# One buffer class for outputs and relu results, one for inputs and inverse decays, three-chunk channel weights, and a new instruction order in a linear-attention plus mixer kernel

## The chip, the cores and the metric

The kernel runs on one core of one Trainium2 chip. The metric is the device time of one execution in microseconds (us), the median of several runs. The engines are named as in the profile: PE is TensorE, DVE is VectorE, ACT is ScalarE, POOL is GpSimd, SP is SyncE, which here only issues transfers. PEld is the weight load of TensorE.

## What is computed

A gated linear attention (a state that decays by `alpha` at each step) gives `x`; an MLP mixer, first over tokens and then over channels, follows. There are 4 batches, 8 heads of 48 and 768 time steps.

```python
for t in range(S):
    state = alpha[:, :, t, :, None] * state + np.einsum('bhd,bhe->bhde', k[:, :, t], v[:, :, t])
    y[:, :, t] = np.einsum('bhd,bhde->bhe', q[:, :, t], state)
...
h = np.maximum(xt @ w_tok1, 0.0) @ w_tok2          # 768 -> 256 -> 768 over tokens
u = x + h.transpose(0, 2, 1)
h2 = np.maximum(u @ w_ch1, 0.0) @ w_ch2            # 384 -> 1536 -> 384 over channels
return (u + h2).astype(np.float32)
```

## The kernel before

**Attention.** The 12 chunks of 256 time steps (3 to a batch, numbered 0 to 11, the last part of each step's name) are worked one after the other. A partition holds two successive steps. Of a chunk the four inputs `at` (alpha), `kt`, `qt` and `vt` are loaded by `ld_at`, `ld_kt`, `ld_qt`, `ld_vt`, 384 KB each. `ln` takes the logarithm, `cum` (in chunks 0 to 2 the wider `cumw`) sums it along the steps by matmul, `E` and `IE` are its exponential and the inverse of that, `kk` and `qq` scale the keys and queries by them, `trk`/`trq` transpose these on PE (chunks 0 to 5; later `dk`/`dq` do it by transfer) and `evk`/`evq` (`pq`) bring them to SBUF. `G` is the product of keys and queries for each half chunk (`G0_`, `G1_`), `mask` its causal mask on DVE, `K` the state's increment, made from the key copies `ka`, `kb`, `kc` and the value copies `vb`, `vs0_`, `vs1_`, `sa` and `sm` the new state, `ia`/`ib` the part of the output that comes from the state, `y` the rest, and `x` the copy of the result to SBUF.

**Mixer.** For each batch b, `t1_b_m_c` multiplies by `w_tok1`, `ht` is its relu, `t2_b_i` multiplies by `w_tok2`, `u_b_i` adds x, `up`/`ut` (batch 0) or the transfer `ux` (others) transposes u, `c1_b_mc_half` multiplies by `w_ch1` for one of 12 column chunks `mc` and one half of the time steps, `rt` is its relu, `c2_b_i_q` sums over `w_ch2` in four parts, `o_b_i` adds u, and `st_b_i` stores 128 steps. The weights come in as 16 loads `ldw` of 384 KB into the same buffers as the inputs, and a cast `cw` brings each to bf16: 2 of `wt1`, 2 of `wt2`, 6 of `wc1`, 6 of `wc2`.

**What sets the order.** `build` writes down every step with what it reads and writes. `ORDER` is a table of step names; the letter at a name's end is the engine (t PE, s ACT, v DVE, g POOL, y SP). Each engine runs its own steps strictly in the order in which they stand there. `BUFS` gives the number of the buffer for each value at its first use, within its class; `CLASSES` says how many each class has. A step waits by semaphores for what it reads and for the last user of a buffer that it overwrites. In `ORDER` a load stands shortly before its first reader, so it says nothing of when the load runs: SP runs through its loads, as far as buffers are free.

**Fillers.** Steps `fN_name` are matmuls on zeros with no use but to keep PE at work, worth N matmuls of 512 columns, put ahead of the step `name` in batch 0's stretch.

**A shared port.** Steps marked `port=True` (products on SBUF operands and casts) are chained over DVE and POOL: `shared` makes one of them on DVE wait for the last one before it on POOL in `ORDER`, and the other way round.

Lines that the profile names: L584 loads inputs, L600 to L607 the weights, L624 stores; L637/L631/L634 are the logarithms, L687/L679 `IE`, L683/L676 `E`; L700 `kk` and `qq`; L712 `trk`/`trq`; L643 is every other small matmul, fillers (`ps<-rt`) included; L746 and L745 copies and casts; L770 `mask`; L841 and L844 `sa` and `sm`; L878, L883, L902 and L907 are `t1`, `t2`, `c1` and `c2`; L875/L873 the relus; L887 `u`; L894 `up`; L911 `o`.

What a channel product waits for before is said by two lines: for chunks 0 to 5 three weight pieces, for chunks 6 to 11 the three others.

```python
reads=[ut], preds=(uts[0:2 + half] if b in UP else [uts[half]]) + [wl[("wc1", p)] for p in ((0, 1, 2) if mc < 6 else (3, 4, 5))],
```

Of the kernel before, what the change touches and what calls it, by code (L numbers as in the profile page):

```python
# [8 lines left out]
F32 = mybir.dt.float32  # L9
# [54 lines left out]
class Plan:  # L64
# [5 lines left out]
    def val(self, cls, name=""):  # L70
        return Val(cls, name)
# [30 lines left out]
UP = (0,)  # L102
# [5 lines left out]
    "in": 19,  # L108
    "la": 2, "lf": 2, "E": 3, "IE": 2, "pkq": 2, "pkk": 3, "vb": 3,
    "tpk": 4, "tpq": 2, "gtm": 2, "tmp": 2, "ss": 4, "kt": 1, "x": 9, "ht": 3, "u": 4, "ut": 2, "rt": 20, "o": 3,  # L110
}
WIDE = (0, 1, 2)
# [8 lines left out]
def build(g):  # L121
# [185 lines left out]
    wl = {}  # L307
# [8 lines left out]
    def mixer(b):  # L316
# [56 lines left out]
        for i in range(NS):  # L373
            hold = 4000.0 if (i >= NS - 3 and b < B - 1) else 0.0
            cuts = [(0, HD // 2), (HD // 2, HD)] if (b, i) == LAST else [(0, HD)]
            for ci, (ca, cz) in enumerate(cuts):
                nm = f"{b}_{i}" if len(cuts) == 1 else f"{b}_{i}h{ci}"
                bank, o_ = V("one"), V("o")
# [31 lines left out]
ld_at1y ld_at0y ln1s ln0s f8_cumw1t f1_cumw1t cumw1t IE1s cumw0t IE0s ld_vt0y E0s vb0g vs0_0g vs1_0v ld_kt0y kk0v  # L410
f8_trk0t f1_trk0t trk0t E1s ld_qt0y qq0v ka0s kb0s kc0v f1_trq0t trq0t ld_kt1y kk1v K0t evq0s s0_0v ld_vt1y vb1s
f1_trk1t trk1t ld_at2y evk0v ln2s f2_G0_0t G0_0t ld_qt1y ka1g sa1_0v f4_cumw2t cumw2t mask0_0v vs0_1s kb1g kc1g vs1_1s
K1t sm1_0g qq1v sa0_1v sm0_1v G1_0t ld_kt2y IE2s E2s trq1t evq1s ib0t mask1_0v f3_y1_0t y1_0t y0_0t evk1v G0_1t sa1_1v
ld_qt2y x1_0s mask0_1v G1_1t ld_vt2y x0_0s vb2s kk2g trk2t kc2s ldw_wt10y qq2g cw_wt10s f2_ia1t ia1t mask1_1v evk2s
trq2t ld_at3y vs1_2g ldw_wt11y evq2v ib1t y1_1t y0_1t vs0_2g ldw_wt21y sm1_1g P3g K2t sa0_2v sm0_2g x0_1s t1_0_0_0t
f1_G0_2t G0_2t ldw_wt20y G1_2t cw_wt20g t1_0_1_0t mask0_2v x1_1s t1_0_1_1t ld_at4y ld_kt3y t1_0_1_2t lnP3s cum3t
cw_wt11s IE3s ia2t y0_2t x0_2s t1_0_0_1t t1_0_0_2t E3s t1_0_0_3t mask1_2v t1_0_1_3t ib2t y1_2t ldw_wc14y t1_0_1_4t
x1_2s t1_0_0_4t f1_t1_0_1_5t t1_0_1_5t ht_0_1v P4g cw_wt21s t1_0_0_5t ht_0_0s f3_t2_0_0t t2_0_0t t2_0_1t u_0_0v ln13s
r13s ldw_wc13y t2_0_2t u_0_1v t2_0_3t u_0_2v t2_0_5t lnP4s t2_0_4t u_0_3v u_0_5v u_0_4v up_0_0t cw_wc14s cw_wc13s
# [74 lines left out]
class Emit:  # L494
# [76 lines left out]
    def t(self, v):  # L571
        return self.T[v.cls][v.buf]
# [393 lines left out]
```

## Time and profile before

| | us |
|---|---|
| median of 3 runs | 162.97 (162.54 to 163.51) |
| span of the profiled execution | 160.5 |
| PE busy in that span | 154.6 (96%) |
| DVE busy | 114.9 (72%) |
| ACT busy | 97.8 (61%) |
| POOL busy | 80.8 (50%) |
| c1, L902, 288 matmuls, busy | 50.3 |
| c2, L907, 300 matmuls, busy | 52.4 |
| fillers, L643 `ps<-rt`, 29 matmuls, busy | 12.1 |

The span goes from the first to the last instruction of the program in one profiled execution; the device time of a run also holds what lies around it. The ends of matmuls are modelled, so a small pause between two matmuls does not show as idle time; the difference of two starts does show it. HBM is read for 25.17 MB and written for 4.72 MB. Over the first 100 us the 16 transfer engines are busy nearly all the time, at some 320 GB/s.

### The profile page before, as it was taken

The page shows a single profiled execution, that of the slowest core. Times are in us where ns is not written, and L with a number is a line of the kernel's source. Part 1 is how long each engine was busy: PE and PEld are TensorE (multiplying, and loading weights), DVE is VectorE, ACT ScalarE, POOL GpSimd, SP SyncE. Part 2 cuts the span into 40 slices and gives each one's busy share as a digit, 9 for nine tenths or more (in the row PEclk, how much of TensorE's full clock was granted, in tenths as well). Part 3 has the DMA queues.
Part 4 walks back from the last instruction along what each step waited for, and adds up shares of the span by engine and source line. Part 5 has one row for each costly group of instructions (what it writes and reads, how often), then busy time and mean ns, then how long its engine had stood idle before and what let it go on. Part 6 is the DMA issues. An engine that isn't in the chain of part 4 may idle for free.

```text
span 160.5 us, 3971 instructions
## 1 busy us (share of the span) xinstructions
PE 154.6 (96%) x1563; PEld 97.1 (60%) x1563; DVE 114.9 (72%) x206; ACT 97.8 (61%) x179; POOL 80.8 (50%) x94
## 2 busy tenths in 40 slices
PE   7999989999999999999999999999999999999992
PEld 2545565766667676666667666566567665665661
DVE  6099994979889787989969758795886762464222
ACT  3789999998899955897563583269832203343000
POOL 5205897695973649389778852699523000000000
PEclk9999999999999999999999999999999999999999
DMA  4999999999999999999989999989701235111133
GB/s 122 320 324 317 317 374 311 339 333 306 316 347 324 275 278 272 210 228 319 241 202 298 239 315 204 217 196 134 196 21 62 87 79 169 49 49 53 49 129 116
DMA packets 76130, 35.05 MB, mean 218 GB/s; under 512 B 70352, under 2 KB 74320, under 8 KB 76112
## 3 DMA queue, kind: packets, MB, share of 16 engines
q1 hardware_dynamic: 73808, 31.76, 74.1%
q10 hardware_dynamic: 2304, 3.05, 5.3%
q8 instruction: 12, 0.20, 0.5%
q14 instruction: 6, 0.05, 0.1%
HBM read 25.17 MB, written 4.72 MB: 186 GB/s over the span
## 4 chain that ended last, share of the span: by engine, by line
PE 61%; DMA 12%; DVE 6%; ACT 6%; SPq 6%; POOL 4%; issue 3%; DVEq 0%; POOLq 0%
PE ps L907 22%; PE ps L902 21%; PE ps L643 11%; DMA in<-in_v_dram 6%; SPq L584 6%; DMA out_dram<-o 4%; PE ps L878 3%; PE ps L883 2%; DMA ut<-u 2%; DVE pkk L700 2%; DVE gtm L770 1%; PE ps L712 1%; DVE rt L875 1%; POOL vb L746 1%; POOL pkq L700 1%
## 5 line engine op out<-in xcount | busy, mean ns | idle before, releaser
L907 PE MATMUL ps<-wc,rt 128*128 128x384 bf16 (+1 forms) x300 | 52.4, 319 | 0.0
L902 PE MATMUL ps<-ut,wc 128*128 128x384 bf16 x288 | 50.3, 326 | 0.1
L902 PEld LDWEIGHTS <-wc 128*128 128x128 bf16 x288 | 27.1, 98 | 17.9 <-DMA ut<-u 0.6
L907 PEld LDWEIGHTS <-rt 128*128 128x128 bf16 x300 | 27.8, 98 | 16.0
L873 ACT ACTIVATE rt<-ps 128x384 bf16<-128x384 f32 x47 | 21.4, 492 | 23.6 <-PE ps L902 23.3
L875 DVE TENSOR_SCALAR rt<-ps 128x384 bf16<-128x384 f32 x49 | 25.6, 551 | 9.1 <-PE ps L902 8.9
L770 DVE TENSOR_TENSOR gtm<-ps,mk 128x1024 bf16<-128x1024 f32 x24 | 28.5, 1218 | 3.1 <-PE ps L643 2.8
L911 DVE TENSOR_TENSOR o<-ps,u 128x384 f32<-128x384 f32 (+1 forms) x25 | 13.2, 536 | 12.6 <-PE ps L907 10.1
L700 POOL TENSOR_TENSOR pkk<-in,IE 128x768 bf16<-128x768 f32 x8 | 14.5, 1817 | 3.3 <-DVE ss L844 2.3
L745 ACT CAST x<-ps 128x384 bf16<-128x384 f32 x20 | 9.2, 479 | 11.1 <-PE ps L643 9.5
L887 DVE TENSOR_TENSOR u<-ps,x 128x384 bf16<-128x384 f32 x24 | 12.0, 550 | 3.1 <-PE ps L883 2.5
L746 POOL CAST vb<-in 64x384 bf16<-64x384 f32 (+1 forms) x14 | 8.3, 594 | 10.4 <-DMA in<-in_v_dram 4.7
L692 POOL TENSOR_TENSOR in<-in,in 128x384 f32<-128x384 f32 x8 | 8.0, 1000 | 10.5 <-DVE u L887 3.8
L643 PE MATMUL ps<-rt 128*128 128x512 bf16 (+1 forms) x29 | 12.1, 515 | 1.1 <-DVE rt L541 1.1
L745 ACT CAST vb<-in 64x384 bf16<-64x384 f32 (+1 forms) x18 | 11.4, 634 | 0.8 <-DMA in<-in_v_dram 0.3
L700 POOL TENSOR_TENSOR pkq<-in,E 128x768 bf16<-128x768 f32 x6 | 10.9, 1818 | 0.6 <-DMA tpk<-pkq 0.3
L878 PE MATMUL ps<-x,wt 128*128 128x384 bf16 x48 | 11.0, 325 | 0.0
L844 POOL TENSOR_TENSOR ss<-tmp,E 128x384 bf16<-128x384 f32 x10 | 8.3, 833 | 4.2 <-DVE in L628 3.9
L841 DVE TENSOR_TENSOR tmp<-ps,ss 128x384 f32<-128x384 f32 x16 | 8.8, 552 | 1.8 <-PE ps L643 0.6
L883 PE MATMUL ps<-ht,wt 128*128 128x384 bf16 x48 | 9.1, 326 | 0.0
L643 PE MATMUL ps<-vb,gtm 128*128 128x48 bf16 x192 | 8.2, 183 | 0.2 <-DVE gtm L770 0.2
L643 PE MATMUL ps<-tpq,tpk 48*64 48x128 bf16 (+1 forms) x288 | 7.9, 218 | 0.4 <-POOL tpq L746 0.3
(94 smaller groups left out, 207.6 us busy)
## 6 DMA issues: line engine op xcount, KB each, us to landing
in<-in_alpha_dram SPq DMA_DIRECT2D x12, 384.0 KB, 5.1
in<-in_v_dram SPq DMA_DIRECT2D x12, 384.0 KB, 5.6
in<-in_k_dram SPq DMA_DIRECT2D x12, 384.0 KB, 5.2
in<-in_q_dram SPq DMA_DIRECT2D x12, 384.0 KB, 5.5
in<-in_moe_w_ch_dram SPq DMA_DIRECT2D x12, 384.0 KB, 5.9
out_dram<-o ACTq DMA_DIRECT2D x15, 192.0 KB, 1.8
in<-in_moe_w_tok_dram SPq DMA_DIRECT2D x4, 384.0 KB, 6.0
out_dram<-o SPq DMA_DIRECT2D x8, 192.0 KB, 2.2
```

The costliest lines, as they stand in the source:

```text
L643: return self.pe.matmul(out, lhsT=lhsT, rhs=rhs, start=start, stop=stop, skip_group_check=True)
L700: self.shared(self.eng[e].tensor_tensor(self.t(dst)[:, :, h0:h1, 0:D], self.t(src)[:, h0:h1].rearrange("p h s d -> p s h d"), bass.AP(tens ...
L745: return self.act.copy(d, s)
L770: self.nc.vector.tensor_tensor(self.t(gtm)[:, hf, :, :], self.pair(gp).rearrange("p a (j t) -> p (a j) t", t=128), bass.AP(tensor=m.tensor ...
L873: self.act.activation(d, s, AF.Relu)
L875: self.nc.vector.tensor_scalar_max(d, s, 0.0)
L878: self.pe.matmul(self.bank(bank)[:, 0:HD], lhsT=self.wt1[:, kc, m * 128 : m * 128 + 128], rhs=self.t(x), start=(kc == 0), stop=(kc == NS - 1))
L883: self.pe.matmul(self.bank(bank)[:, 0:HD], lhsT=self.wt2[:, kc, i * 128 : i * 128 + 128], rhs=self.t(hts[kc]), start=(kc == 0), stop=(kc = ...
L887: self.nc.vector.tensor_tensor(self.t(u)[:, i % 3], self.bank(bank)[:, 0:HD], self.t(x), ALU.add)
L902: self.pe.matmul(self.bank(bank)[:, 0:HD], lhsT=self.wc1[:, kc, mc * 128 : mc * 128 + 128], rhs=self.t(ut)[:, 3 * half : 3 * half + 3, kc, ...
L907: self.pe.matmul(self.bank(bank)[:, 0 : cz - ca], lhsT=self.t(rts[mc][0])[:, i * 128 : i * 128 + 128], rhs=self.wc2[:, mc, ca:cz], start=( ...
L911: self.nc.vector.tensor_tensor(self.t(o)[:, ca:cz], self.bank(bank)[:, 0 : cz - ca], self.t(u)[:, i % 3, ca:cz], ALU.add)
```

## The change

**Buffer classes.** The class `o` (3 outputs of 384 fp32) goes into `rt` (768 bf16, the same size), which grows from 20 to 23. The class `IE` (2) goes into `in`, which grows from 19 to 21. The sums stay the same; `Plan.val` does it by an alias, and `t` and the new `o` give the tile in the shape that is wanted.

**Weight pieces.** A piece of `wc1` was 128 rows by 768 columns (one 3072-byte run to a partition) and is now all three row chunks by 256 columns (three runs of 1024 bytes); so `c1` of chunk mc waits for piece mc // 2 alone. A piece of `wt2` was 128 rows by 768 columns and is now both row chunks by 384 columns; so `t2` of block i waits for piece i // 3 alone.

**Order.** `ORDER`, `BUFS` and so every engine's sequence are new. Fillers go from 13 steps worth 36 matmuls of 512 columns to 9 steps worth 26. Stores go from 16 on ACT and 9 on SP to 12 and 13, and all stores of batch 0 now stand in the last third of the table.

```diff
 CLASSES = {
-    "in": 19,
-    "la": 2, "lf": 2, "E": 3, "IE": 2, "pkq": 2, "pkk": 3, "vb": 3,
-    ... "u": 4, "ut": 2, "rt": 20, "o": 3,
+    "in": 21,
+    "la": 2, "lf": 2, "E": 3, "pkq": 2, "pkk": 3, "vb": 3,
+    ... "u": 4, "ut": 2, "rt": 23,
 }
+ALIAS = {'o': 'rt', 'IE': 'in'}
+PAIRED = ()
...
-                     reads=[h for h, _ in hts], preds=[h for _, h in hts] + [wl[("wt2", p)] for p in range(2)],
+                     reads=[h for h, _ in hts], preds=[h for _, h in hts] + [wl[("wt2", i // 3)]],
...
-                         reads=[ut], preds=(...) + [wl[("wc1", p)] for p in ((0, 1, 2) if mc < 6 else (3, 4, 5))],
+                         reads=[ut], preds=(...) + [wl[("wc1", mc // 2)]],
...
 ORDER = """
-ld_at1y ld_at0y ln1s ln0s f8_cumw1t f1_cumw1t cumw1t IE1s cumw0t IE0s ld_vt0y E0s vb0g vs0_0g vs1_0v ld_kt0y kk0v
...
+ld_kt0y ld_at0y ld_at1y ln0s f12_cumw0t f2_cumw0t cumw0t ld_at2y ln1s cumw1t IE0s kk0v f2_trk0t trk0t E0s ld_qt0y qq0v trq0t ln2s
...
         elif nm == "wt2":
-            self.gated(dma(t, self.w[1][128 * piece : 128 * piece + 128, :]), op)
+            w = self.w[1].rearrange("(c p) m -> p c m", p=128)
+            self.gated(dma(t.rearrange("p (c m) -> p c m", c=2), w[:, :, HD * piece : HD * piece + HD]), op)
         elif nm == "wc1":
-            c, h = piece % 3, piece // 3
-            self.gated(dma(t, self.w[2][128 * c : 128 * c + 128, 768 * h : 768 * h + 768]), op)
+            w = self.w[2].rearrange("(c p) m -> p c m", p=128)
+            self.gated(dma(t.rearrange("p (c m) -> p c m", c=3), w[:, :, 256 * piece : 256 * piece + 256]), op)
```

**Where the order moves things: SP at the start.** The first eleven loads; a row reads "buffer <- input in HBM, shape". Before:

```order
L584 DMA in_75<-in_alpha_dram 128x8x96
L584 DMA in_72<-in_alpha_dram 128x8x96
L584 DMA in_76<-in_v_dram 128x8x96
L584 DMA in_64<-in_k_dram 128x8x96
L584 DMA in_65<-in_q_dram 128x8x96
L584 DMA in_72<-in_k_dram 128x8x96
L584 DMA in_69<-in_v_dram 128x8x96
L584 DMA in_73<-in_alpha_dram 128x8x96
```

After:

```order
L600 DMA in_64<-in_k_dram 128x8x96
L600 DMA in_65<-in_alpha_dram 128x8x96
L600 DMA in_67<-in_alpha_dram 128x8x96
L600 DMA in_70<-in_alpha_dram 128x8x96
L600 DMA in_69<-in_q_dram 128x8x96
L600 DMA in_65<-in_v_dram 128x8x96
L600 DMA in_67<-in_k_dram 128x8x96
L600 DMA in_71<-in_q_dram 128x8x96
```

Chunk 0's keys now come first and its alpha second (before: chunk 1's alpha, chunk 0's alpha, chunk 0's values); the alphas of chunks 1 and 2 are third and fourth.

**DVE in chunks 0 to 2.** In these rows `gtm` is a mask's result, `tpq` `evq`'s, `tpk` `evk`'s, `pkk` and `pkq` are `kk`'s and `qq`'s, `tmp` and `ss` the state's. Before, the last rows ahead of the first `ht`:

```order
L841 TENSOR_TENSOR tmp_110<-ps,ss_112 128x384
L844 TENSOR_TENSOR ss_113<-tmp_110,E_89 128x384
L770 TENSOR_TENSOR gtm_107<-ps,mk 128x1024
L746 COPY tpk_102<-ps 128x2x8x64
L841 TENSOR_TENSOR tmp_109<-ps,ss_113 128x384
L770 TENSOR_TENSOR gtm_108<-ps,mk 128x1024 x2
L746 COPY tpq_105<-ps 128x2x512
L841 TENSOR_TENSOR tmp_109<-ps,ss_114 128x384
L770 TENSOR_TENSOR gtm_107<-ps,mk 128x1024 x2
```

After:

```order
L859 TENSOR_TENSOR tmp_109<-ps,ss_111 128x384
L788 TENSOR_TENSOR gtm_107<-ps,mk 128x1024
L788 TENSOR_TENSOR gtm_108<-ps,mk 128x1024
L718 TENSOR_TENSOR pkk_96<-in_74,in_70 128x16x48
L788 TENSOR_TENSOR gtm_107<-ps,mk 128x1024
L859 TENSOR_TENSOR tmp_110<-ps,ss_112 128x384
L788 TENSOR_TENSOR gtm_108<-ps,mk 128x1024
L859 TENSOR_TENSOR tmp_109<-ps,ss_113 128x384
L788 TENSOR_TENSOR gtm_107<-ps,mk 128x1024
L859 TENSOR_TENSOR tmp_110<-ps,ss_114 128x384
L788 TENSOR_TENSOR gtm_107<-ps,mk 128x1024
```

DVE gives up one `sm` (to POOL) and chunk 2's `evq` (to ACT) and takes chunk 2's `kk` (from POOL); that product now reads its inverse decays from an `in` buffer, `in_70`.

**DVE where the first channel products start.** Before, the rows from the last `u` on:

```order
L887 TENSOR_TENSOR u_128<-ps,x_119 128x384
L746 COPY ut_131<-ps 128x768 x2
L875 TENSOR_SCALAR rt_134<-ps 128x384
L875 TENSOR_SCALAR rt_133<-ps 128x384
L875 TENSOR_SCALAR rt_144<-ps 128x384 x2
```

After:

```order
L764 COPY ut_131<-ps 128x768
L718 TENSOR_TENSOR pkk_94<-in_64,in_80 128x16x48
L893 TENSOR_SCALAR rt_135<-ps 128x384
L764 COPY ut_131<-ps 128x768
L893 TENSOR_SCALAR rt_136<-ps 128x384
L893 TENSOR_SCALAR rt_134<-ps 128x384
L893 TENSOR_SCALAR rt_133<-ps 128x384
L718 TENSOR_TENSOR pkq_93<-in_66,E_89 128x16x48
L764 COPY kt_97<-pkk_94 64x8x48
L764 COPY pkk_94<-pkk_94 64x8x48
```

Chunk 3's `kk` and `qq` (two products of 768) and two of its key copies now run on DVE among the first relus; before, `kk3` and `qq3` ran on POOL and these copies on POOL and ACT.

More of the change, by code (lines that the diff above doesn't have):

```diff
@@ L107 @@
 CLASSES = {
[L108 to L111 removed]
+    "in": 21,
+    "la": 2, "lf": 2, "E": 3, "pkq": 2, "pkk": 3, "vb": 3,
+    "tpk": 4, "tpq": 2, "gtm": 2, "tmp": 2, "ss": 4, "kt": 1, "x": 9, "ht": 3, "u": 4, "ut": 2, "rt": 23,
+}
+ALIAS = {'o': 'rt', 'IE': 'in'}
+PAIRED = ()
 WIDE = (0, 1, 2)
@@ L377, in mixer @@
                 nm = f"{b}_{i}" if len(cuts) == 1 else f"{b}_{i}h{ci}"
-                bank, o_ = V("one"), V("o")
+                bank = V("one")
+                if b not in PAIRED:
+                    o_ = V("o")
+                elif i % 2 == 0:
+                    o_ = V("in")
                 prev = None
@@ L415 @@
[L415 to L419, printed above, removed]
```

159 lines of the change are left out of this document (87 added, 72 removed), and 22 rows, old and new, of the table BUFS.

## The prediction

> **What bounds the kernel now.** I read the page's first block, a table of windows, PE's sequence over the first 32 us, then what DVE, ACT and POOL waited for there. First the span, PE's share and the windows (PE, PEld, DVE, ACT, POOL busy, granted clock, transfer share, GB/s).
>
> ```profile
> span 160.5 us, 3971 instructions
> PE 154.6 (96%) x1563; PEld 97.1 (60%) x1563; DVE 114.9 (72%) x206; ACT 97.8 (61%) x179; POOL 80.8 (50%) x94
> 8.00:16.00 8.00, 7.72 (x84) 4.07 (x83) 7.51 (x11) 7.27 (x11) 2.64 (x5) 1.00 1.16 321
> 16.00:24.00 8.00, 7.14 (x115) 4.80 (x114) 7.71 (x10) 7.38 (x13) 6.97 (x7) 1.00 1.11 346
> 24.00:31.76 7.76, 7.73 (x87) 4.84 (x86) 5.43 (x10) 7.41 (x14) 5.72 (x6) 1.00 1.03 322
> 31.76:60.00 28.24, 28.14 (x305) 18.76 (x306) 24.26 (x38) 24.70 (x43) 18.35 (x22) 1.00 1.04 312
> 60.00:100.00 40.00, 40.00 (x432) 25.66 (x431) 33.11 (x58) 26.09 (x55) 29.25 (x27) 1.00 1.03 254
> 100.00:130.00 30.00, 29.64 (x336) 18.94 (x335) 23.00 (x37) 14.24 (x28) 14.78 (x16) 1.00 0.56 124
> 130.00:157.40 27.40, 27.40 (x181) 17.09 (x179) 10.83 (x21) 6.42 (x14) 0.00 (x0) 1.00 0.28 90
> ```
>
> From 31.76 us, where c1 starts, to 157.4 PE idles 0.10 + 0 + 0.36 + 0 = 0.46 us: that part is a solid block of matmuls, and an order can win half a microsecond there, or lose. What an order can change is when the block starts. PE's rows before it, and the waits that ended its idle time later (waits, windowed from 31.8 us):
>
> ```profile
> 1.06 4.21 PE L643 MATMUL ps<-rt 128*64 128x384 f32 x7 [1.06 <-DVE rt L541]
> 5.17 0.71 PE L643 MATMUL ps<-la,u 128*128 128x384 bf16 x3
> 7.34 2.26 PE L643 MATMUL ps<-rt 128*64 128x384 f32 x7
> 27.73 2.28 PE L883 MATMUL ps<-ht,wt 128*128 128x384 bf16 x12
> 30.81 0.61 PE L712 MATMUL ps<-idn,pkk 128*128 128x128 bf16 x8
> 31.25 0.50 PE L894 MATMUL ps<-idn,u 128*128 128x128 bf16 x6
> 31.76 4.55 PE L902 MATMUL ps<-ut,wc 128*128 128x384 bf16 x27
> PE ps L643 <- POOL tpq L746: 0.3, 1, 0.3
> PEld L902 <- DMA ut<-u: 0.6, 2, 0.5
> ```
>
> PE looks busy before 31.76 too, but partly with fillers (36 units of 512 columns). In the windows from 8 to 24 us DVE is busy 15.2 of 16 us: DVE's chain carries chunks 0 to 2, and the fillers hide PE's waiting for it. DVE's rows:
>
> ```profile
> 8.33 0.35 DVE L746 CAST vb<-in 64x384 bf16<-64x384 f32 x1 [4.26 <-POOL vb L746]
> 8.72 0.96 DVE L700 TENSOR_TENSOR pkk<-in,IE 128x768 bf16<-128x768 f32 x1
> 9.59 0.95 DVE L700 TENSOR_TENSOR pkq<-in,E 128x768 bf16<-128x768 f32 x1
> 10.57 0.26 DVE L746 COPY pkk<-pkk 64x384 bf16<-64x384 bf16 x1
> 17.76 0.68 DVE L746 COPY tpk<-ps 128x1024 bf16<-128x1024 bf16 x1
> 18.36 0.55 DVE L841 TENSOR_TENSOR tmp<-ps,ss 128x384 f32<-128x384 f32 x1
> 21.30 1.30 DVE L746 COPY tpq<-ps 128x1024 bf16<-128x1024 bf16 x1
> 22.52 0.53 DVE L841 TENSOR_TENSOR tmp<-ps,ss 128x384 f32<-128x384 f32 x1
> 23.17 2.36 DVE L770 TENSOR_TENSOR gtm<-ps,mk 128x1024 bf16<-128x1024 f32 x2
> 28.27 2.88 DVE L887 TENSOR_TENSOR u<-ps,x 128x384 bf16<-128x384 f32 x6 [0.83 <-PE ps L883]
> 31.06 0.55 DVE L746 COPY ut<-ps 128x768 bf16<-128x768 bf16 x1
> ```
>
> The last mask ends at 25.53 (23.17 + 2.36). After it come y, x, the last t1, ht, t2 at 27.73 and six u; c1 starts 4.03 us after t2. Last, the loads and ACT:
>
> ```profile
> 4.28 0.84 ACT L637 ACTIVATE la<-in 128x768 bf16<-128x768 f32 x1 [2.19 <-DMA in<-in_alpha_dram]
> 5.47 0.84 ACT L637 ACTIVATE la<-in 128x768 bf16<-128x768 f32 x1 [0.35 <-DMA in<-in_alpha_dram]
> 6.32 0.81 ACT L687 ACTIVATE IE<-ps 128x768 f32<-128x768 f32 x1
> 26.37 0.83 ACT L745 CAST wt<-in 128x768 bf16<-128x768 f32 x1
> 27.10 0.49 ACT L873 ACTIVATE ht<-ps 128x384 bf16<-128x384 f32 x1
> 6.91 1.39 POOL L746 CAST vb<-in 128x768 bf16<-128x768 f32 x2 [4.11 <-DMA in<-in_v_dram]
> 24.76 0.82 POOL L746 CAST wt<-in 128x768 bf16<-128x768 f32 x1 [0.56 <-DMA in<-in_moe_w_tok_dram]
> 30.16 0.88 POOL L746 CAST wc<-in 128x768 bf16<-128x768 f32 x1 [0.36 <-DMA in<-in_moe_w_ch_dram]
> ```
>
> Loads land one by one: the 1st, 2nd and 3rd at 4.28, 5.47 and 6.9, the 17th (`wt20`) at 24.76, the 22nd (`wc15`, the third piece that c1 waits for) at 30.16. From the 1st to the 17th that is 1.28 us apart, to the 22nd 1.08.
>
> **The change part by part.**
>
> *Weight pieces.* c1's first chunk needs one piece, the 20th load in the new order: 24.76 + 3 x 1.08 = 28.0, cast by 28.9 (0.88). Before, the third piece was cast at 31.04. That wait goes; late next is u's transpose on DVE, which stands at 31.61 before (31.06 + 0.55). So the pieces alone bring at most 0.15 us (31.76 - 31.61). The runs of 1024 bytes cost nothing or a little: `wt1` has such runs already and lies inside the 1.28 spacing; even 0.2 us each would put the sixth piece 1.2 us later, at a place where 2 us are left.
>
> *The start.* Chunk 0's alpha is the 2nd load: ln ends at 5.47 + 0.84 = 6.31. The fillers ahead are 14 units, not 9: 9 take 4.11 us cold (1.06 to 5.17), and warm 2.26, that is 0.25 each; so 5.17 + 5 x 0.25 = 6.4 and `cumw0` starts at 6.4, where `cumw1` started at 5.17. It ends 1.1 later, at 7.5 (5.17 to ACT's 6.32 before). ACT does chunk 1's ln first (3rd load: 6.9 to 7.7), so `IE0` runs 7.6 to 8.44 and DVE's first product starts at 8.48: 0.24 us before 8.72.
>
> *DVE's chain.* Prices are the steps from one start to the next: product of 768 0.87, evk 0.60, a copy on 64 partitions 0.26 to 0.35, state step 0.47, mask 1.18, evq 1.22. The new list up to the last mask is 5 products, 2 evk, 4 such copies, 5 state steps, 6 masks: 4.35 + 1.2 + 1.2 + 2.35 + 7.1 = 16.2. Before it was 16.4 with 0.8 of waits on top. Step by step I find 0.3 of waits in the new one (for POOL's key copy, the value cast, chunk 1's copies): 8.48 + 16.2 + 0.3 = 25.0, against 25.53. ACT takes chunk 2's evq and still has it done 1 us before it is used; were that cover gone, the masks of chunk 2 would be late by as much. `wt2`'s last cast no longer stands ahead of ht on ACT (26.37 to 27.10), worth 0.1: t2 at 27.05, and c1 4.0 us later, at 31.05. That is 0.7 earlier.
>
> *What is given back.* `trk3` stood before c1 (30.81 to 31.25, 0.44) and stands behind it now. The same PE work remains otherwise, so the block ends 0.70 - 0.44 = 0.26 earlier.
>
> *The block.* Of its 0.46 us idle, 0.36 lie at 100 to 117 us: u's transposes of batch 2 and the last `pq` on POOL. Before, two c1 blocks of the other half (0.49 each, 4.55 / 27 x 3 less the last's pipe) stand on PE ahead of the first reader of the transpose that came late, now six, 1.9 us more; the last `pq` moves to ACT, and its transfer is issued some 8 us of PE work, counted in the new table, ahead of the reader. I take both away. Bounds: nothing to -0.46 for what goes; for new waits 0 to 2.5 (below).
>
> *Buffers and stores.* DVE's o group, and the window behind the last matmul:
>
> ```profile
> L911 DVE TENSOR_TENSOR o<-ps,u 128x384 f32<-128x384 f32 (+1 forms) x25 | 13.2, 536 | 12.6 <-PE ps L907 10.1 <-DMA out_dram<-o 2.5
> 157.40:160.60 3.20, 0.01 (x1) 0.00 (x0) 0.36 (x1) 0.00 (x0) 0.00 (x0) 1.00 0.26 92
> ```
>
> Outputs in `rt` and `IE` in `in` remove no work. The waits for an output's landing, 2.5 us on DVE, lay where PE did not wait. ACT issues 4 stores fewer, SP 4 more; the SP ones stand behind transfers that come earlier, and nothing of a later batch queues behind them. Late stores share the transfer engines with nothing else (share 0.28 from 130 us). The end after the last matmul, 3.1 us, stays; were the late stores to queue, up to 0.5 each.
>
> Sum: -0.70 + 0.44 - 0.36 = -0.62, so 159.9 for the span. The median before, 162.97, lies 2.4 above the span; the forecast is 162.3. No change could be told from one within 0.5%, 0.8 us.
>
> **The rivals.**
>
> 1. *DVE, loaded with chunk 3's products, holds PE in the first c1 (slower).* From 30.3 to `evq3` DVE now has 2 transposes' copies, 2 products, 6 relus, 2 key copies and evq: 1.05 + 1.74 + 6 x 0.48 + 0.6 + 1.22 = 7.5, and relus that wait for PE; I get 38.6, and PE reaches chunk 3's `G` at 38.7. POOL's cast of `wc15` waits for DVE's key copies by the shared port and is due 0.4 us later. So each microsecond that DVE slips beyond some 0.4 stands on PE. At 1.8 us of slip PE waits 1.4, and 162.3 becomes 163.8, slower; at 2.4, 164.3. For it: no slack, and DVE busy 24.3 of 28.2 in that window already. Against: the same window held PE for only 0.10 us before, with ACT just as full. 0.22.
>
> 2. *The start gains more (faster).* PE's new list has 10 filler units (2.2 us) and `trk3` less before c1. If PE's list, not DVE, sets c1's start, the block ends 2.2 earlier and with the 0.36 the time is 160.4. For it: PE busy 7.73 of 7.76 before c1. Against: DVE's 15.2 of 16. 0.13.
>
> 3. *The longer filler outlasts the logarithm.* The granted clock reads 1.00 throughout, yet the same 7 matmuls take 4.21 us first and 2.26 at 7.34: PE starts cold, and is warm at 5.17. If it stays cold, 14 units take 14 x 0.457 = 6.4 and end at 7.5, 1.1 late, and DVE's chain with it: 163.4. Against: it was warm in time in this execution. 0.13. The Trainium skill ("TensorE: Matmul & The Clock Gate", Part 1) says that the gate opens after about one window of 3.4 us of activity, a window that runs free, so that the moment varies by some 0.5 us. By that rule the filler would end at 6.65 at worst, an estimate from its 0.5 us, and the sum would be 0.25 us higher, not 1.1; the trace agrees in that the fast rate is there 4.1 us after the first matmul.
>
> **How the numbers follow.** Forecast 0.52, rivals 0.22, 0.13, 0.13. The forecast's own range is 161.7 (c1 0.4 earlier still, all idle gone) to 162.8 (no idle won): nearly half of it, 0.24, lies under 162.15. So faster 0.24 + 0.13 = 0.37, slower rival 1 with 0.22, the same 0.41 (the rest of the forecast, rival 3). The range goes from 160.6, which takes in most of rival 2, to 164.4, the top of rival 1.
>
> **What would show it.** Right: the first `pkk` product on DVE near 8.5, the last mask ending near 25.0, the first L902 near 31.05, idle of PE in 100 to 130 below 0.1, 3.1 us after the last matmul. Wrong: L902 at 29 (rival 2) or 32 (rival 3), PE idle over 1 us between 32 and 60 with DVE as releaser (rival 1), or waits for stores or transfers in the block.

## The result, and the profile after

The changed kernel takes 162.03 us (median of 22 runs, 161.21 to 163.23), the kernel before in the same rounds 162.81 us (22 runs, 162.08 to 164.35). The ratio is 0.9943, 95% interval 0.9922 to 0.9965: faster by 0.6%, about 0.9 us. A ratio leaves out executions more than 1.5% above the fastest of their kernel, so it can differ a little from the quotient of the medians. Its profiled execution has a span of 160.3 us and a device time of 162.03, so 1.7 lies around the span.

The first block of the page, and the windows of the changed kernel (columns as before: length; PE, PEld, DVE, ACT, POOL busy; granted clock; transfer share; GB/s). c1 starts at 30.84, the last matmul ends at 157.14.

```profile
span 160.3 us, 3961 instructions
PE 152.1 (95%) x1555; PEld 96.6 (60%) x1555; DVE 115.0 (72%) x205; ACT 99.1 (62%) x183; POOL 75.9 (47%) x91
8.00:16.00 8.00, 6.55 (x81) 3.92 (x80) 7.49 (x13) 7.80 (x10) 2.26 (x2) 1.00 1.17 327
16.00:24.00 8.00, 6.89 (x125) 5.00 (x125) 8.00 (x10) 7.82 (x14) 5.94 (x10) 1.00 1.12 351
24.00:30.84 6.84, 6.38 (x76) 4.11 (x74) 4.68 (x10) 5.01 (x12) 5.81 (x7) 1.00 1.05 321
30.84:60.00 29.16, 29.16 (x324) 19.83 (x325) 26.87 (x41) 25.04 (x47) 17.44 (x20) 1.00 1.03 297
60.00:100.00 40.00, 39.52 (x417) 25.03 (x415) 30.54 (x52) 26.92 (x55) 27.55 (x28) 1.00 0.95 213
100.00:130.00 30.00, 29.96 (x340) 19.16 (x338) 22.97 (x37) 16.03 (x32) 14.82 (x15) 1.00 0.70 150
```

Three things are to be seen. From 8 to 24 us DVE is busy 15.5 of 16 us (before 15.2), and ACT now 15.6 (before 14.7). PE's idle time of 0.36 at 100 to 130 is gone (0.04). And there is a new one of 0.48 at 60 to 100, where before had none. (The rate of some 320 GB/s given above for the first 100 us holds for the first 60 only: from 60 to 100 us it was 254 before and is 213 now.) PE's and DVE's rows at the start, which answer to those of before:

```profile
1.05 5.10 PE L661 MATMUL ps<-rt 128*64 128x384 f32 x10 [1.05 <-DVE rt L547]
6.41 0.65 PE L661 MATMUL ps<-la,u 128*128 128x384 bf16 x3 [0.26 <-ACT la L655]
26.71 2.11 PE L901 MATMUL ps<-ht,wt 128*128 128x384 bf16 x12
30.84 1.14 PE L920 MATMUL ps<-ut,wc 128*128 128x384 bf16 x6
31.81 0.61 PE L730 MATMUL ps<-idn,pkk 128*128 128x128 bf16 x8
```

```profile
8.34 0.96 DVE L718 TENSOR_TENSOR pkk<-in,in 128x768 bf16<-128x768 f32 x1 [4.27 <-ACT in L705]
23.43 1.22 DVE L788 TENSOR_TENSOR gtm<-ps,mk 128x1024 bf16<-128x1024 f32 x1
30.14 0.55 DVE L764 COPY ut<-ps 128x768 bf16<-128x768 bf16 x1
```

DVE's first product starts at 8.34 (before 8.72), the last mask ends at 24.65 (25.53), t2 starts at 26.71 (27.73), c1 at 30.84 (31.76). The new idle time is at 88 to 91 us. The waits of PE from 84 to 100 us (engine, line, releaser; total, times, longest), and ACT's row before the first of them:

```profile
PE ps L661 <- ACT tpq L763: 0.2, 1, 0.2
PE ps L661 <- ACT la L652: 0.2, 1, 0.2
```

```profile
87.28 1.35 ACT L763 COPY tpq<-tpk 128x1024 bf16<-128x1024 bf16 x1 [0.44 <-DMA tpk<-pkq]
```

The ACT row is `pq8`: it waits 0.44 us for the transfer `dq8`, and with it PE waits for `G0_8`; the logarithm `lnP9`, behind it on ACT, holds `cum9`. That transfer was issued at 80.35; here are the transfers that were issued from 80 to 84 us, with their median time from issue to landing.

```profile
tpk<-pkq SPq DMA_TRANSPOSE x1, 6.9
tpk<-pkk SPq DMA_TRANSPOSE x1, 4.5
```

### The profile page after: what moved, and what is told of

Its sections match the earlier page's. It is cut to its first block, busy times and chain, and to the rows that moved or that the text cites. A ratio compares the mean times of both kernels' runs of the same rounds, so it can differ in the third digit from the quotient of the medians.

```text
span 160.3 us, 3961 instructions
## 1 busy us (share of the span) xinstructions
PE 152.1 (95%) x1555; PEld 96.6 (60%) x1555; DVE 115.0 (72%) x205; ACT 99.1 (62%) x183; POOL 75.9 (47%) x91
## 4 chain that ended last, share of the span: by engine, by line
PE 75%; ACT 7%; DMA 6%; DVE 6%; issue 3%; POOL 1%; SPq 1%; DVEq 0%; POOLq 0%
PE ps L920 29%; PE ps L925 25%; PE ps L661 9%; PE ps L896 5%; PE ps L901 4%; DMA in<-in_alpha_dram 3%; DMA in<-in_v_dram 3%; PE ps L730 2%; ACT vb L763 2%; DVE u L905 2%; DVE pkq L718 1%; DVE pkk L718 1%; ACT tpq L763 1%; ACT x L763 1%; DVE tmp L859 1%
## 5 line engine op out<-in xcount | busy, mean ns | idle before, releaser
L925 PE MATMUL ps<-wc,rt 128*128 128x384 bf16 (+1 forms) x300 | 53.2, 319 | 0.0
L891 ACT ACTIVATE rt<-ps 128x384 bf16<-128x384 f32 x55 | 25.4, 490 | 25.2 <-PE ps L920 20.2
L893 DVE TENSOR_SCALAR rt<-ps 128x384 bf16<-128x384 f32 x41 | 21.2, 553 | 13.6 <-PE ps L920 13.0
L929 DVE TENSOR_TENSOR rt<-ps,u 128x384 f32<-128x384 f32 (+1 forms) x25 | 13.4, 538 | 9.9 <-PE ps L925 9.6
L862 POOL TENSOR_TENSOR ss<-tmp,E 128x384 bf16<-128x384 f32 x12 | 10.0, 836 | 15.0 <-DVE tmp L859 9.6
L718 POOL TENSOR_TENSOR pkq<-in,E 128x768 bf16<-128x768 f32 x7 | 12.7, 1815 | 6.7 <-DVE pkq L718 3.4
L763 ACT CAST x<-ps 128x384 bf16<-128x384 f32 x17 | 8.1, 477 | 11.8 <-PE ps L661 11.8
L718 DVE TENSOR_TENSOR pkk<-in,in 128x768 bf16<-128x768 f32 x8 | 7.7, 956 | 6.3 <-ACT in L705 4.3
L710 POOL TENSOR_TENSOR in<-in,in 128x384 f32<-128x384 f32 x9 | 9.0, 1002 | 5.1 <-DVE pkq L718 3.8
L661 PE MATMUL ps<-rt 128*128 128x512 bf16 (+1 forms) x21 | 8.9, 528 | 1.1 <-DVE rt L547 1.1
```

The source lines that it names most:

```text
L661: return self.pe.matmul(out, lhsT=lhsT, rhs=rhs, start=start, stop=stop, skip_group_check=True)
L718: self.shared(self.eng[e].tensor_tensor(self.t(dst)[:, :, h0:h1, 0:D], self.t(src)[:, h0:h1].rearrange("p h s d -> p s h d"), bass.AP(tens ...
L763: return self.act.copy(d, s)
L891: self.act.activation(d, s, AF.Relu)
L893: self.nc.vector.tensor_scalar_max(d, s, 0.0)
L925: self.pe.matmul(self.bank(bank)[:, 0 : cz - ca], lhsT=self.t(rts[mc][0])[:, i * 128 : i * 128 + 128], rhs=self.wc2[:, mc, ca:cz], start=( ...
```

## The experiments

A table of the first stage in the single profiled executions comes first, since the experiments lean on it (us; from PE's and DVE's rows):

| profile of | first sum on PE starts | DVE's first product | last mask ends | c1 starts |
|---|---|---|---|---|
| before | 5.17 | 8.72 | 25.53 | 31.76 |
| after | 6.41 | 8.34 | 24.65 | 30.84 |
| after_again | 6.40 | 8.32 | 24.62 | 30.81 |
| stores_early | 6.38 | 8.30 | 24.61 | 30.79 |
| vt8_dk6 | 6.56 | 8.49 | 24.78 | 30.97 |
| vt8_early | 6.78 | 8.71 | 24.99 | 31.18 |
| calm | 7.11 | 9.03 | 25.85 | 32.05 |

The last six have the same instructions up to 31 us. One profile can thus stand 1.2 us from another of the same code, and the verdicts below go by 10 to 12 runs of each kernel, not by spans. The experiments were made in four groups, each with the kernel before run beside it; kernels of different groups are therefore compared by their ratios to it.

**The changed kernel again (after_again, no edit).**

> The changed kernel once more, with a second profile. If the new wait at 88 us (PE idle 0.48 us between 60 and 100 us, for the last query copy of batch 2's third chunk and for the logarithm of chunk 9) belongs to the order, it is there again, 0.3 to 0.6 us, with the transfer dq8 landing 6 us or more after its issue; if it was an accident of one execution, PE idles under 0.1 us there and the span is 159.8 instead of 160.3. Either way c1 (L920) starts at 30.8 +- 0.2 and the ratio to the kernel before is 0.993 to 0.997.

Measured: 162.44 us (12 runs), ratio 0.9964 (0.9930 to 0.9998), span 159.7. Its windows, and the same two transfers as above:

```profile
60.00:84.00 24.00, 24.00 (x219) 14.65 (x217) 18.15 (x32) 16.53 (x33) 17.16 (x16) 1.00 0.89 196
84.00:100.00 16.00, 16.00 (x205) 10.76 (x203) 13.05 (x22) 11.05 (x24) 10.36 (x12) 1.00 0.97 226
100.00:130.00 30.00, 29.83 (x339) 19.10 (x338) 22.86 (x39) 15.27 (x31) 14.85 (x15) 1.00 0.64 147
```

```profile
tpk<-pkq SPq DMA_TRANSPOSE x1, 4.8
tpk<-pkk SPq DMA_TRANSPOSE x1, 4.7
```

c1 starts at the same place, but the wait at 88 us is not there (16.00 of 16.00), and `dq8` lands 4.8 us after its issue instead of 6.9. So the wait belongs to the execution, not to every one: the order leaves no slack there, and a transfer that lands late shows at once. Of four later profiles with the same order at that place, two have the same wait (long_fill 0.57 us, evq2_dve 1.03, with `dq8` at 6.7 and 7.3) and two have none (no_late_fill and fill9, 5.2 and 5.3).

**Chunk 2's query copy back on DVE (evq2_dve).**

```diff
-evq2s
+evq2v
```

> The changed kernel with chunk 2's query copy (evq2) put back from ACT to DVE, at the same place in the order. Theory (DVE's chain through chunks 0 to 2 sets the start of c1): DVE's copy costs 1.22 us, the later masks slip by 1.0 to 1.2 us, c1 starts at 31.8 to 32.0 instead of 30.84, and the time is 0.9 to 1.2 us above that of the changed kernel. Rival (PE's own list, shorter by fillers and trk3, sets the start): c1 stays within 0.2 us of 30.84 and the time within 0.3 us.

Measured: 164.41 us (10 runs), ratio 1.0077 (1.0040 to 1.0114). DVE's last mask and PE's first c1:

```profile
24.63 1.21 DVE L788 TENSOR_TENSOR gtm<-ps,mk 128x1024 bf16<-128x1024 f32 x1
32.42 1.14 PE L920 MATMUL ps<-ut,wc 128*128 128x384 bf16 x6
```

The last mask ends 1.19 us later, as DVE's chain says, and c1 starts 1.58 later (the other 0.39 comes between t2 and c1). The first DVE product starts where it did (8.33 against 8.34), so the delay is not one of this execution's start. The time is 1.1% above that of the changed kernel, 1.8 us: more than expected, since PE also idles 1.02 us at 60 to 100 and 0.45 at 100 to 130 in this profile. DVE's chain sets the start; the rival, that PE's list does, falls.

**The same step alone, in the kernel before (b_evq2).**

```diff
-evq2v
+evq2s
```

> The kernel before with one step alone done as in the changed kernel: chunk 2's query copy (evq2) on ACT instead of DVE, at its old place in the order. Theory (the move pays only together with the new order of the steps around it): ACT takes it behind evk2, from 22.5 to 23.9 us by its rows before, where DVE had it done at 22.6, so chunk 2's G and masks come 1.0 us later, c1 starts 0.7 to 1.1 us later and the time rises by that. Rival (DVE's chain is the limit wherever it is lightened): DVE has 1.22 us less, c1 starts 0.5 to 1.2 us earlier and the time falls by that.

Measured: 164.26 us (10 runs), ratio 1.0064 (1.0025 to 1.0102). On ACT the copy runs behind evk2, and DVE's masks wait for it:

```profile
23.30 1.30 ACT L745 COPY tpq<-ps 128x1024 bf16<-128x1024 bf16 x1
```

```profile
25.16 2.36 DVE L770 TENSOR_TENSOR gtm<-ps,mk 128x1024 bf16<-128x1024 f32 x2 [1.13 <-PE ps L643]
```

In this profile c1 starts at 33.83, 2.07 us later than before and more than the theory's 0.7 to 1.1; the median is some 1.0 higher. The step that is worth 1.1% in the new order costs 0.6% in the old one, where ACT has another copy to do first.

**The kernel before with the new weight pieces alone (b_pieces).** `wc1` and `wt2` as in the change, the old order, and the three right pieces of `wc1` loaded in the order 5, 4, 3.

```diff
-[wl[("wc1", p)] for p in ((0, 1, 2) if mc < 6 else (3, 4, 5))]
+[wl[("wc1", mc // 2)]]
-ldw_wc14y ... ldw_wc13y ... ldw_wc15y
+ldw_wc15y ... ldw_wc14y ... ldw_wc13y
```

> The kernel before, in its own order, with only the new weight pieces: wc1 in three-chunk pieces (each c1 waits for one piece), wt2 by columns, and the three pieces of the right half of wc1 loaded in the order in which c1 asks for them. Prediction's step (late next is u's transpose on DVE, at 31.61): c1 starts at 31.61 to 31.76 and the time is 0 to 0.15 us below that of the kernel before. Rival (the pieces carry the start's gain): c1 starts at 31.0 or earlier and the time falls by 0.6 us or more.

Measured: 163.44 us (12 runs), ratio 1.0026 (0.9994 to 1.0057). The last cast of the three on POOL, u's transpose on DVE and c1:

```profile
31.03 0.88 POOL L746 CAST wc<-in 128x768 bf16<-128x768 f32 x1 [1.49 <-DMA in<-in_moe_w_ch_dram]
```

```profile
31.17 0.55 DVE L746 COPY ut<-ps 128x768 bf16<-128x768 bf16 x1
```

```profile
31.87 1.30 PE L902 MATMUL ps<-ut,wc 128*128 128x384 bf16 x7
```

c1 starts at 31.87, before the third piece's cast ends (31.91) and 0.15 behind the transpose's copy (31.72): the old wait is gone, and the transpose is late next. The pieces alone bring no gain that can be measured.

**No fillers behind the first two (no_late_fill).**

```diff
-f2_trk0t ... f1_K0t ... f1_trk1t ... f3_G0_1t ... f1_G0_0t ... f2_G0_2t ... f2_t2_0_2t
```

> The changed kernel without the seven filler steps behind the first two (12 units of 512 columns, some 2.5 us of PE). Theory (DVE's chain sets the start): PE's idle time before c1 grows by the 2.5 us, c1 starts within 0.2 us of 30.84 and the time is within 0.3 us. Rival A (PE's list sets it): c1 starts 1 to 2.5 us earlier and the time falls as much. Rival B (PE loses its fast rate when it idles more): matmuls between 8 and 31 us become slower, c1 starts 0.5 us or more later and the time rises by that.

Measured: 162.61 us (10 runs), ratio 0.9976 (0.9942 to 1.0010), within 0.2 us of the changed kernel's second set: by the time, the theory. The profile shows rival B beside it:

```profile
12.00:16.00 4.00, 2.21 (x37) 1.61 (x35) 3.96 (x8) 3.82 (x5) 1.38 (x1) 1.00 1.17 328
16.00:20.00 4.00, 3.55 (x48) 2.81 (x49) 3.91 (x4) 3.60 (x7) 2.46 (x4) 0.57 1.10 364
```

After 4 us in which PE is busy 2.2, the granted clock is 0.57 for the next 4. c1 starts at 32.03 there, against 30.8; 0.4 of that comes from a late first sum (the filler outlasts the logarithm there). This is no accident of one execution: over the whole span the mean granted clock is 0.986 to 0.989 in 8 of the 10 runs (median of these 162.67 us), and 1.00 in the two others, which took 161.75 and 162.14. All 34 runs of the changed kernel have at least 0.996. So PE's list does not set the start (rival A falls), and what the 12 units buy is the clock. By the two ratios they are worth 0.2 us, which is less than the intervals can tell from nothing.

**The first filler longer and shorter (long_fill, fill9).**

```diff
-f12_cumw0t f2_cumw0t
+f12_cumw0t f6_cumw0t      (long_fill: 18 units)
+f8_cumw0t f1_cumw0t       (fill9: 9 units)
```

> The changed kernel with the first filler 4 units longer (18 instead of 14). In nine profiles so far PE left its half rate between 4.3 and about 7 us, so 14 units end between 6.0 and 7.1 and chunk 0's logarithm at 6.36: the filler is already the later of the two in some executions. Theory (the first sum of chunk 0, and with it DVE's chain and c1, starts when the filler ends): 18 units end between 6.9 and about 8.2, the first sum starts 0.5 to 1.1 us later than in the same execution with 14, and the time rises by 0.5 to 1.1 us (ratio to the kernel before 0.999 to 1.003). Rival (there is slack between the first sum and DVE's chain, or PE is warm for the transposes that follow and gains it back): the time within 0.3 us of the changed kernel.

> The changed kernel with the first filler 5 units shorter (9, as many as the kernel before has there). Theory (the filler outlasts the logarithm only in executions in which PE warms up late): there the first sum starts at 6.4 instead of 6.8 to 7.1 but runs itself at half rate (0.5 us more), and where PE warms up early nothing changes: the time is 0 to 0.2 us lower. Rival A (14 units are always in the way): 0.3 to 0.7 us lower. Rival B (PE idles 0.5 to 1.4 us ahead of the first sum and loses or misses its fast rate): matmuls up to 12 us at half rate, and the time 0.3 us or more higher.

Measured: long_fill 163.05 us (10 runs), ratio 0.9985 (0.9944 to 1.0026); fill9 162.31 us (12 runs), ratio 0.9943 (0.9906 to 0.9979). PE's first rows of long_fill, of fill9, and of calm (below), whose first filler is that of the changed kernel:

```profile
1.05 5.89 PE L661 MATMUL ps<-rt 128*64 128x384 f32 x12 [1.05 <-DVE rt L547]
6.88 0.66 PE L661 MATMUL ps<-la,u 128*128 128x384 bf16 x3
```

```profile
1.06 4.22 PE L661 MATMUL ps<-rt 128*64 128x384 f32 x7 [1.06 <-DVE rt L547]
6.38 1.12 PE L661 MATMUL ps<-la,u 128*128 128x384 bf16 x3 [1.10 <-ACT la L655]
```

```profile
1.05 6.21 PE L661 MATMUL ps<-rt 128*64 128x384 f32 x10 [1.05 <-DVE rt L547]
7.11 0.65 PE L661 MATMUL ps<-la,u 128*128 128x384 bf16 x3
```

Four units more put the first sum at 6.88 and c1 at 31.30, 0.47 and 0.46 later than in the profile of after, one for one. By the ratio the time is 0.3 us above after_again and 0.7 above the first set: the direction of the theory, though the interval reaches down to no difference. Five units fewer change nothing in the time. In the profile the sum starts at 6.38 but itself runs at half rate (three matmuls in 1.12 us, against 0.65), and c1 starts at 31.42, 0.58 later than after, which is rival B in this one execution. In calm the same 10 filler matmuls take 6.21 us instead of 5.10, and the sum starts 0.70 late: the prediction's third rival, in single executions.

**The stores of batch 0 early again (stores_early).** Each `st_0_i` two ACT steps behind its `o_0_i`, on ACT.

```diff
-st_0_3s ... st_0_5s st_0_2s ... st_0_4y ... st_0_1s ... st_0_0s   (112 to 150 us)
+st_0_5s st_0_3s st_0_0s st_0_4s st_0_1s st_0_2s                   (55 to 70 us)
```

> The changed kernel with the six stores of batch 0 put behind their outputs again (on ACT, some 55 to 70 us), instead of in the last third. Prediction's step (late stores cost and bring nothing, since the waits for an output's landing lay where PE did not wait): the time is within 0.3 us of the changed kernel. Rival (the late stores leave the transfer engines free for the loads and transposes of 60 to 117 us, which is where the shared buffer class brings its gain): the transposes dq6 to dq8 land 0.5 to 2 us later, PE idles 0.3 us or more in addition between 60 and 120, and the time rises by 0.3 to 1.0 us.

Measured: 163.83 us (10 runs), ratio 1.0085 (1.0046 to 1.0124), 1.2% above after_again, 2.0 us; the only effect of like size is evq2_dve's 1.1%. c1 of batch 0 starts at 30.79, as before; the loss is in the block. The window, the waits of PE and of its weight load (60 to 100), ACT's row before PE's wait, and the transfers issued from 60 to 95 us:

```profile
60.00:84.00 24.00, 22.46 (x193) 13.52 (x195) 16.37 (x30) 14.88 (x31) 15.77 (x15) 1.00 0.95 223
```

```profile
PE ps L661 <- ACT tpq L763: 0.9, 1, 0.9
```

```profile
PEld L920 <- DMA ut<-u: 1.0, 1, 1.0
```

```profile
79.64 1.34 ACT L763 COPY tpq<-tpk 128x1024 bf16<-128x1024 bf16 x1 [3.01 <-DMA tpk<-pkq]
```

```profile
tpk<-pkq SPq DMA_TRANSPOSE x3, 6.3
ut<-u SPq DMA_TRANSPOSE x2, 4.1
```

The same rows of the changed kernel, and of the kernel before:

```profile
tpk<-pkq SPq DMA_TRANSPOSE x3, 5.2
ut<-u SPq DMA_TRANSPOSE x2, 2.9
```

```profile
tpk<-pkq SPq DMA_TRANSPOSE x3, 2.7
ut<-u SPq DMA_TRANSPOSE x2, 3.0
```

With the stores beside them the transposes of u take 4.1 us to landing instead of 2.9, and the `dq` 6.3 instead of 5.2. The first c1 of batch 1 waits 1.0 for u's transpose, and PE 0.9 for `pq6`, whose ACT copy waits 3.0 for `dq6` (7.2 us from issue to landing). The rival holds, at twice its price. But stores in this stretch do not cost that everywhere: in the kernel before, five of batch 0's six stores are issued between 56.9 and 79.6 us too, and there u's transposes take 3.0, the `dq`, which do not stand right behind loads there, 2.7, and PE idles 0 from 60 to 100. There they go out one at a time; here the last four go out as two pairs, at 64.6 and 65.0 beside u's transposes and at 69.7 and 70.0 ahead of `dq6`. So the 2.0 us is the price of these places in the new order, not the gain over the kernel before; whether the pairing makes the difference was not tried.

**The readers of late transfers put later (calm).**

```diff
-ld_vt8y vb8g dq8y ... cum9t ... c2_1_0_3t ... G1_10t ... c2_2_2_0t c2_2_2_1t
+vb8g dq8y ld_vt8y ... c2_1_0_3t cum9t ... c2_2_2_0t c2_2_2_1t G1_10t
```

> The changed kernel with three steps moved in the order: the transfer dq8 ahead of the load ld_vt8 on SP's queue, the product c2_1_0_3 ahead of cum9 on PE, and c2_2_2_0 and c2_2_2_1 ahead of G1_10 on PE, so that the steps that read pq8, lnP9 and pq10 come later. Theory (what is left idle in the block, 0.48 and 0.06 us over two profiles at 88 to 91 us and 0.04 and 0.17 at 113, and a part of the spread between executions, comes from transfers that land late against a fixed place in the order): PE idles less than 0.1 us from 60 to 130 us, and the time falls by 0.2 to 0.5 us against the changed kernel, with fewer slow executions. Rival (the waits move to the next reader, or the spread comes from elsewhere): the idle time stays at 0.2 us or more in other places and the time within 0.2 us.

Measured: 163.18 us (12 runs, none under 162.59), ratio 1.0011 (0.9982 to 1.0040): slower than the changed kernel by 0.5%, against the theory. PE's idle time moved and grew:

```profile
60.00:100.00 40.00, 39.54 (x433) 25.20 (x431) 31.00 (x53) 26.85 (x54) 26.39 (x27) 1.00 0.96 213
100.00:130.00 30.00, 29.48 (x340) 18.80 (x339) 22.71 (x37) 16.03 (x33) 16.36 (x17) 1.00 0.68 152
```

```profile
PE ps L661 <- DVE gtm L788: 0.5, 1, 0.5
PE ps L661 <- DMA tpk<-pkk: 0.3, 1, 0.3
```

`dq8` now lands 4.6 us after its issue (6.9 and 4.8 in the two profiles of the changed kernel), but `dk8`, behind the load, 5.8 instead of 4.5 and 4.7, and chunk 8 needs both; and PE waits 0.5 us for a mask, probably since `G1_10`, with c2 put ahead of it, feeds its mask later.

**The load moved to where transfers are idle (vt8_early, vt8_dk6).** The buffer of `ld_vt8` is free from 50 us. vt8_dk6 moves `dk6` and one more load besides.

```diff
-ld_vt6y dk6y ux_1_0y ux_1_1y ld_at10y ld_qt7y ... ld_vt7y ld_vt8y dq8y
+ld_vt6y ld_vt8y dk6y ux_1_0y ux_1_1y ld_at10y ld_qt7y ... ld_vt7y dq8y   (vt8_early)
+ld_vt6y ld_vt8y ux_1_0y ux_1_1y dk6y ld_qt7y ld_at10y ... ld_vt7y dq8y   (vt8_dk6)
```

> The changed kernel with one load moved on SP's queue: ld_vt8 (free buffer since 50 us, issued at 79.6) right behind ld_vt6, so that it runs at 63 to 65 us, where the transfer share is 0.04, instead of ahead of dq8 and dk8. Theory (chunk 8's transposes are late because a load of 384 KB stands ahead of them): dq8 and dk8 are issued 0.6 us earlier and land about 1.2 us earlier, by 86 and 87, PE idles under 0.1 us at 84 to 100 instead of 0 to 0.9, and the time falls by 0.2 to 0.6 us. Rival (the load pushes u's transposes ux_1_0 and ux_1_1, which land at 67.0 just when c1 of batch 1 wants them at 67.1): PE waits 0.3 to 1.2 us at 67, and the time is the same or up to 0.6 us higher.

> As the kernel with ld_vt8 moved, and besides dk6 (landed at 65.5, read at 79) behind ux_1_1, and the load ld_qt7 ahead of ld_at10, so that nothing new stands ahead of u's transposes. Theory: no wait at 67, none at 84 to 100, and the time 0.3 to 0.6 us below that of the changed kernel, also below that of the one with the load moved alone if its ux lands late. Rival (dk6 and the loads behind it, 1.3 us later, delay chunk 7's queries or kc6): new waits of 0.2 to 0.8 us of PE between 75 and 83 us, and the time no lower than that of the changed kernel.

Measured: vt8_early 162.15 us (12 runs), ratio 0.9941 (0.9907 to 0.9974); vt8_dk6 162.98 us (12 runs), ratio 0.9986 (0.9956 to 1.0016). vt8_early from 84 to 100 us, its transfers issued from 80 to 84, and vt8_dk6 from 60 to 84:

```profile
84.00:100.00 16.00, 15.98 (x202) 10.60 (x201) 12.73 (x22) 11.05 (x23) 10.34 (x12) 1.00 0.84 213
```

```profile
tpk<-pkq SPq DMA_TRANSPOSE x1, 4.7
tpk<-pkk SPq DMA_TRANSPOSE x1, 3.1
```

```profile
60.00:84.00 24.00, 22.65 (x206) 13.84 (x208) 16.73 (x30) 15.13 (x31) 16.14 (x15) 1.00 0.98 215
```

In vt8_early `dk8` takes 3.1 us to landing, against 4.5 and 4.7 in the two profiles of the changed kernel, and PE does not wait. `dq8` takes 4.7, against 6.9 and 4.8, so it is no sooner than in after_again, where PE did not wait either: the profile does not show the theory. Nor can the ratio be told from the changed kernel's (0.9943 and 0.9964). In vt8_dk6 `dq6`, pushed back, lands 6.5 us after its issue, and PE waits 1.4 us for its copy: the rival's kind of wait, and longer. No version here beats the changed kernel by a margin that was measured.

One more order (start3), with two of DVE's products and some copies on POOL and ACT, moves steps in the first 31 us so that part of what they compute is changed; it is told for its start alone.

> The changed kernel with another order up to the first channel products alone: chunk 0's alpha is the first load, kk0 and kk2 and some copies go from DVE to POOL or ACT, two casts and relus are dealt out anew; the fillers keep their number. Theory (DVE's chain from the first load to the last mask sets the start of c1, and the block behind it follows): DVE has 1.9 us less work in 8 to 24 us and begins 1.2 us earlier, c1 starts at 29.8 +- 0.3, and the time falls by 0.6 to 1.0 us against the changed kernel. Rival A (the loads, one each 1.2 us, set what comes next): c1 starts earlier but PE waits 0.5 us or more between 30 and 60 us for weight pieces or chunk 3, and the time falls by less than 0.4 us. Rival B (PE, busy only 36% at 8 to 10 us, falls to its slow rate): the time rises.

Measured: 164.13 us (10 runs), ratio 1.0067 (1.0031 to 1.0104), c1 at 32.01. Chunk 0's logarithm ends at 5.18, but the first sum starts only behind the filler, at 6.34; then DVE's first product (`qq0`) waits for POOL's `kk0`, which takes 1.81 us where DVE takes 0.96, and starts at 10.17. None of the gain arrives.

## Why the prediction was right, and where it was not

- **Median.** Forecast 162.3 in 160.6 to 164.4; measured 162.03 and, in the second set, 162.44. The difference of 0.62 us forecast stands against 0.93 (ratio 0.9943) and 0.58 (0.9964). The prediction's border between "faster" and "the same" lay at 0.995, between the two sets.
- **Offset: luck.** I set the median 2.4 above the span; the changed kernel's profiled run has 162.03 for 160.3, so 1.7. The forecast span was 159.9. So the span was forecast 0.4 too short and the offset 0.7 too large, and that the sum of both comes near is luck. With 1.7 the profiled execution of before took some 162.2, an estimate, and was a quick one, 0.6 under the median of 22.
- **Weight pieces: at most 0.15 us.** Right as far as the interval tells: alone they gave 1.0026 (0.9994 to 1.0057), with u's transpose late next, as said.
- **The start, -0.70.** Right in its mechanism, a little small: 31.76 to 30.84 is -0.92 between these two profiles. Each mark came 0.1 to 0.4 early (first product 8.34 for 8.48, last mask 24.65 for 25.0, t2 26.71 for 27.05, c1 30.84 for 31.05). The term that was mis-sized is the 0.3 us of waits that I had put into DVE's new list: from first product to last mask it took 16.3, against 16.2 without waits, and DVE is busy 8.00 of 8.00 from 16 to 24. evq2_dve shows that the copy on ACT carries this gain, and b_evq2 that it does so in this order and not in the old one. The other moves of the start were not tried one by one.
- **`trk3`, +0.44.** Seen as said: it stands at 31.81, behind the first c1 steps, and 0.45 us until the next c1.
- **The block, -0.36 at 100 to 117.** Idle of PE from 100 to 130 fell to 0.04 in one profile and 0.17 in the other.
- **No new waits, taken as 0 within bounds of 0 to 2.5.** Wrong in one of the two profiles: 0.48 us at 88 to 91. I had counted the slack of the last `pq`, and not that of `dq8`, which stands behind two loads on SP. In the profiled execution it ate the rest: -0.92 + 0.44 - 0.10 - 0.32 + 0.48 = -0.42 against a measured -0.26 (the last matmul, 157.40 to 157.14). The 0.16 between them may lie in pauses too short to show as idle; that is not shown.
- **Late stores cost nothing.** True, and it misses the point: with the new order the places of batch 0's stores matter. Put early again they cost 2.0 us, since transposes stand beside them. The step that failed is "remove no work", where I asked only who waits for a store's landing and not what a store delays. The shared class lets batch 0's outputs stay until 112 to 150 us; no run has the new order without it, so what the class itself is worth stays open.
- **Rivals.** Rival 1 (DVE holds PE in the first c1) did not come: PE idles 0 at 30.84 to 60. (Its sum is off by 0.1: 162.3 and 1.4 make 163.7.) Rival 2 (PE's list sets the start) falls with evq2_dve and no_late_fill. Rival 3 (the filler outlasts the logarithm) is real in single executions, 0.15 to 0.7 us of late first sum in four of the eight profiles that have the 14 units ahead of it; its sign, c1 at 32, came in calm (32.05), with 0.5 of the delay from another cause. It is probably part of the spread of 161.2 to 163.2. Since the new order gained more than it lost, the median does not show it. The end after the last matmul stayed at 3.2.

What stays open: how often each of the three lateness sources (PE's rate, a late load, a late transpose) strikes; a profile shows one execution at a time.

## What to carry to other kernels

Ask of a buffer change what it lets be done later, and of a store what stands beside it: here batch 0's stores, put back beside transposes, cost 1.2%, though stores in the same stretch cost nothing visible in the old order. A step moved to another engine has no price of its own; the same copy was worth 1.1% in one order and cost 0.6% in another, so read who stands ahead of it there. Before fillers are taken out, look at the granted clock of every run and not at the time alone. And where an order is tuned until nothing waits, look at two or three profiles of the same kernel: places without slack show as waits in one and not in the next.

## What was not expected of the hardware

PE's half rate ends at a moment that differs between executions, with the same instructions: the ten filler matmuls took 4.94 us (stores_early), 5.05, 5.10, 5.89 (vt8_early) and 6.21 (calm). In the views the granted clock reads 1.00 from the start all the same, since the trace's clock record begins only with the fast rate (at 4.65 us in after, at 7.01 in calm). From start to start a filler of 384 columns in fp32 takes 0.64 us at first and 0.32 later; the change comes 3.3 to 5.9 us after the first matmul in the eight profiles with these fillers. The Trainium skill ("TensorE: Matmul & The Clock Gate", Part 1) gives about 3.4 us of activity, and half a microsecond either way for the moment of the change; a spread as small as that these runs do not bear out. It says too that the number of slow matmuls differs from run to run, which they do. The prediction's estimate of 6.65 for the end of the filler at worst, drawn from that spread, was passed in three of them: the first sum starts at 6.78 (vt8_early), 6.80 (no_late_fill) and 7.11 (calm).

The stream of loads, one landing each 1.2 us, has, by the times of landing, one gap of 2.2 to 2.7 us between 15 and 20 us in 11 of 14 profiles (3.2 us in calm). Mostly it falls on a weight; in calm it fell on chunk 2's keys, which took 6.8 us from issue to landing (18.90) instead of 4.8, and DVE stood idle before their product, though its row names no releaser:

```profile
18.98 0.96 DVE L718 TENSOR_TENSOR pkk<-in,in 128x768 bf16<-128x768 f32 x1 [0.51 <-issue]
```

What makes the gap was not tried.
